# A rational activation's denominator without a square, and the order of its quotients, in a two-layer kernel

## The chip, the cores and the metric

One core of a Trainium2 chip. The metric is the time on the device of one execution, in microseconds: the median of several runs. The kernel before took 1278.8 us (three runs, 1276.81 to 1279.39).

## What is computed

The input x has 8192 rows of 192 numbers. A causal convolution of seven taps along the rows (taps from a softmax) comes first. Two layers of the same shape follow, each a product to 2048 hidden numbers, an activation, and a product back to 192. The first activation is h * sigmoid(1.702 h). The second is rational:

```
h = x @ w_in
P = a[0] + a[1]*h + a[2]*h*h + a[3]*h*h*h
Q = 1 + |b[0]|*|h| + |b[1]|*h*h
out = (P / (Q + 1e-6)) @ w_out
```

## The kernel before

The rows are cut into 16 blocks of T = 512 (NB = 16), the hidden numbers into 16 parts of 128 that are handled in NS = 8 steps of two parts, so that a tile of the activation is 128 x 1024. The engines' instructions stand in a fixed order, written out by hand; nothing reorders them.

Three PSUM tiles (`ps_h`) take turns for hidden products, transposes and maxima, and one (`ps_o`) for the output products. A hidden product (`h_product`, L361) splits both sides into high and low halves in f16: six matmuls of the full 128 rows (L371) and six of 64 rows (L381). `o_chunk` (L392) multiplies one 128-part of the activation with its weights, in f16 halves for layer 1 and in f32 for layer 2 (16 matmul instructions for two chunks, L403).

The second activation runs in these passes on each 128 x 1024 tile:

- `terms` (L463): on ScalarE pp = scale*h + bias (L470), sq = h*h (L471) and qq = |scale*h| (L472); on VectorE two passes (L473, L474) that make the cubic P - a[0] out of pp and the hidden product in PSUM. The second gives the PSUM tile back.
- `denominator` (L477): on VectorE qq = sq*scale + qq (L478).
- `log` (L482) and `inverse` (L485): on ScalarE Ln (L483), then a sigmoid of the negative (L486), which together give 1/(1 + qq).
- `quotient` (L488): on VectorE pp = (pp + a[0]) * qq (L489). Its result is what the output product of layer 2 takes.

A pass of the loop over j has two phases. `front_phase` (L564) goes through the eight steps: hidden product and gelu of layer 1 for block j+1 (L420), its high half on GpSimd (L427) and low half on VectorE (L433), hidden product and `terms` of layer 2 for block j, and late output chunks of block j-1. `back_phase` (L595) has the output products of layer 1 for block j+1, the logarithms, the transposed input of block j+3 and its convolution on GpSimd (L297 a product with a tap, L301 the addition), the sigmoids, and then the input of layer 2 for block j+1: `x2_natural` copies it from PSUM (L445, L447), `x2_red` takes its maximum (L452), TensorE broadcasts the maxima (`all_max`, L82), VectorE reduces them (L86), ScalarE writes the high halves (L304) and VectorE the low halves (L307), and `x2_scales` makes columns of scales (L314). The first output chunks of layer 2 end the phase, and the rest goes into lists that the next front phase empties. The end of the phase:

```
        inv(0), inv(1)
        quo(0)
        x2 = x2_natural(n1)
        red = x2_red(x2)
        ...
        inv(2), inv(3)
        scales(pm, sc)
        x2_split(n1, pt, sc)
        quo(1), quo(2), quo(3)
        inv(4), inv(5), inv(6), inv(7)
        chunks[0](), chunks[1]()
        late_pe.extend(chunks[2:])
        late_dve.extend(lambda i=i: quo(i) for i in range(4, NS))
```

In front step i one quotient of `late_dve` is issued before `terms`, and two chunks of `late_pe` after it. The last block has no front phase of its own (`last_phase`, L520): units of hidden product, `terms` and `denominator`, the late work of the block before among them, then the quotients of the first five units, the store of the block before (L498), the last three units, and its own chunks. pp and qq come from rings of eight tiles each, so pp of a block's unit i waits for the chunks of unit i in the block before.

Of the kernel before, what the change touches and what calls it, by code (L numbers as in the profile page):

```python
# [8 lines left out]
F32 = mybir.dt.float32  # L9
# [11 lines left out]
def kernel(  # L21
# [392 lines left out]
    def o2_chunk(n, i, k, g, groups=range(NG)):  # L414
        o_chunk(1, n, NS * k + i, ((g[:, k * T:(k + 1) * T], wo2[:, NS * k + i]),), groups)

    def gelu(n, ph, g=None):
        if g is None:
            g = p2.tile([P, 2 * T], F32, tag="g1", name="g1")
# [3 lines left out]
        return g  # L423

    def g1_high(n, g):
        hl = p2.tile([P, 2, 2 * T], F16, tag="hl", name="hl1", bufs=8)
# [27 lines left out]

    def x2_scales(sc):

        unit = sc[:, 2:3]
        mul(unit, sc[:, 0:1], cst[:, 3:4])
        mul(sc[:, 3:8], ab[:, 8:13], unit)
        mul(sc[:, 5:8], sc[:, 5:8], unit)  # L460
        mul(sc[:, 7:8], sc[:, 7:8], unit)

    def terms(n, ph):  # L463

        sc = sc2_t[n]
        pp = rings[0].tile([P, 2 * T], F32, tag="p", name="pp")
        qq = rings[0].tile([P, 2 * T], F32, tag="q", name="qq")
        sq = p2.tile([P, 2 * T], F32, tag="sq", name="sq")
# [5 lines left out]
        nc.vector.scalar_tensor_tensor(out=pp, in0=pp, scalar=sc[:, 3:4], in1=h, op0=ALU.add, op1=ALU.mult)  # L474
        return pp, qq, sq

    def denominator(n, qq, sq):  # L477
# [4 lines left out]
    def log(qq):  # L482
        nc.scalar.activation(out=qq, in_=qq, func=ACTF.Ln, bias=eps)  # L483

    def inverse(qq):  # L485
        nc.scalar.activation(out=qq, in_=qq, func=ACTF.Sigmoid, scale=-1.0)  # L486

    def quotient(n, pp, qq):  # L488
        nc.vector.scalar_tensor_tensor(  # L489
            out=pp, in0=pp, scalar=ab[:, 0:1], in1=qq, op0=ALU.add, op1=ALU.mult  # L490
        )

    def store(n):
        po = po_t.pop((1, n))
        sc2_t.pop(n)
        t = p1.tile([P, NG, D], F32, tag="on", name="on")
        for k in range(2):
            nc.scalar.activation(  # L498
                out=t[:, 2 * k:2 * k + 2], in_=po[:, k, 0:2 * D].rearrange("p (g d) -> p g d", g=2), func=ACTF.Copy
            )  # L500
        nc.sync.dma_start(out=out[n * T:(n + 1) * T].rearrange("(g p) d -> p g d", p=P), in_=t)
# [3 lines left out]
    def store_half(n, k):  # L505

        if k == 0:
            on_t[n] = p1.tile([P, NG, D], F32, tag="on", name="on")
        t = on_t[n][:, 2 * k:2 * k + 2]
        src = po_t[1, n][:, k, 0:2 * D].rearrange("p (g d) -> p g d", g=2)  # L510
        if k:
            nc.vector.tensor_copy(out=t, in_=src)
        else:
            nc.scalar.activation(out=t, in_=src, func=ACTF.Copy)
# [3 lines left out]
    late_pe, late_dve, early = [], [], {}  # L518

    def last_phase(j):  # L520

        fronts = []

        def units(i, late_q, late_o):
            ph = h_product(1, j, i)
            pp, qq, sq = terms(j, ph)
            for _ in range(late_q):
                late_dve.pop(0)()
            for _ in range(late_o):
                late_pe.pop(0)()  # L530
            denominator(j, qq, sq)
            fronts.append((pp, qq))

        def quotients(steps):
            for i in steps:
                log(fronts[i][1])
            for i in steps:
                inverse(fronts[i][1])
                quotient(j, *fronts[i])

        def own(i):
            for k in range(2):
                o2_chunk(j, i, k, fronts[i][0])

        first = NS // 2 + 1
        for i in range(first):
# [3 lines left out]
        units(first, 0, 0), units(first + 1, 0, 0)  # L550
        own(0)
        units(first + 2, 0, 0)
        for i in range(1, first):
            own(i)
        quotients(range(first, NS))
        for i in range(first, NS - 1):
            own(i)
        for groups in (range(0, 2), range(2, 4)):
            for k in range(2):
                o2_chunk(j, NS - 1, k, fronts[NS - 1][0], groups)  # L560
        store_half(j, 0)
        store_half(j, 1)

    def front_phase(j, n1, extras):  # L564

        fronts, splits = [], []
        for i in range(NS):
            if n1 is not None:
                g = gelu(n1, early.pop((n1, i), None) or h_product(0, n1, i))
                hl = g1_high(n1, g)  # L570
                splits.append(hl)
            if late_dve:
                late_dve.pop(0)()
            if j is not None:
                ph = h_product(1, j, i)
                pp, qq, sq = terms(j, ph)
            for _ in range(2):
                if late_pe:
                    late_pe.pop(0)()
            if n1 is not None:  # L580
                g1_low(n1, g, hl)
            if j is not None:
                denominator(j, qq, sq)
                fronts.append((pp, qq))
            for f in extras.get(i, ()):
                f()
        return fronts, splits
# [7 lines left out]
    def back_phase(j, n1, n2, conv, fronts, splits):  # L595

        for i in range(NS):
            if conv is not None and i == 0:
                x_transpose(conv)
                for k in range(K):  # L600
                    x_conv_pool(conv, k)
            if n1 is not None:
                o1_product(n1, i, splits[i])
            if fronts:
                log(fronts[i][1])
            if conv is not None:
                if i == 5:
                    x_max(conv)
                    x_scales(conv)
                    x_scale_out(conv)  # L610
        inv = lambda i: inverse(fronts[i][1])
        quo = lambda i: quotient(j, *fronts[i])
        chunks = [lambda i=i, k=k: o2_chunk(j, i, k, fronts[i][0]) for i in range(NS) for k in range(2)]
# [3 lines left out]
        inv(0), inv(1)  # L617
        quo(0)
        x2 = x2_natural(n1)
        red = x2_red(x2)  # L620
        sc = sc2_t[n1] = tiny.tile([P, 8], F32, tag="sc2", name="sc2")
        transposes(pt, x2)
        all_max(red, pm)
        inv(2), inv(3)
        scales(pm, sc)
        x2_split(n1, pt, sc)
        quo(1), quo(2), quo(3)
        inv(4), inv(5), inv(6), inv(7)
        chunks[0](), chunks[1]()
        late_pe.extend(chunks[2:])  # L630
        late_dve.extend(lambda i=i: quo(i) for i in range(4, NS))

    def prologue():
# [45 lines left out]
        for c, (src, func) in enumerate(((1, ACTF.Copy), (4, ACTF.Abs), (2, ACTF.Copy), (5, ACTF.Abs), (3, ACTF.Copy))):  # L679
            nc.scalar.activation(out=ab[:, 8 + c:9 + c], in_=ab[:, src:src + 1], func=func)  # L680
# [29 lines left out]
        for i in range(NS):  # L710
            hl = p2.tile([P, 2, 2 * T], F16, tag="hl", name="g0", bufs=8)
            g0.append(gelu(0, h_product(0, 0, i), hl.rearrange("p two t -> p (two t)").bitcast(F32)))
# [38 lines left out]
        sc = sc2_t[0] = tiny.tile([P, 8], F32, tag="sc2", name="sc2")  # L751
# [19 lines left out]
    with tc.manual_schedule():  # L771
        for j in range(NB):
# [16 lines left out]
            if n1 is None:  # L789
                last_phase(j)  # L790
                break
            fronts, splits = front_phase(j, n1, extras)
            back_phase(j, n1, n2, conv, fronts, splits)
# [27 lines left out]
```

## Time and profile before

| | |
|---|---|
| median of three runs | 1278.8 us (1276.81 to 1279.39) |
| the profiled execution | 1279.72 us |
| its span, first to last instruction | 1277.8 us |
| TensorE, matmuls busy | 1215.6 us |
| VectorE busy | 1028.3 us |
| ScalarE busy | 963.0 us |
| GpSimd busy | 606.5 us |

Busy times are of the span of the profiled execution. A matmul's end is modelled, so TensorE's busy time is not its time at the peak rate. An idle time in front of an instruction is put down to what released it last. In a row of the timeline "x16" means sixteen instructions of one line in a row, and the bracket is the engine's idle time before the first.

### The profile page before, as it was taken

Reading aid. Unit: us, or ns where it says so; the run is one execution under the profiler, and the core shown is the slowest. Engines: PE = TensorE matmul, PEld = TensorE weight load, DVE = VectorE, ACT = ScalarE, POOL = GpSimd, SP = SyncE. Lnnn points to the kernel's source line nnn. Section 1 sums busy time; section 2 is a strip of 40 time slices with the busy share of each in tenths; the row PEclk is TensorE's granted clock in tenths of the full one; section 3 lists DMA queues with packets and bytes.
Section 4 is the critical chain, followed back from the end, with each engine's and each line's share of the span. In section 5 each row is a group of like instructions: output and inputs, shape, how many; then the busy total and the mean of one; then the engine's idle time right before and its main releaser. Section 6 shows DMA issues by size and latency. Waiting matters only on the chain.

```text
span 1277.8 us, 20189 instructions
## 1 busy us (share of the span) xinstructions
PE 1215.6 (95%) x8538; PEld 852.8 (67%) x8538; DVE 1028.3 (80%) x1045; ACT 963.0 (75%) x989; POOL 606.5 (47%) x429
## 2 busy tenths in 40 slices
PE   5999999999999999899998999999999999999977
PEld 2564757757685766767676676866767586676766
DVE  6877898796969879696897969789696978968575
ACT  3626977869687786968778697877869787786876
POOL 2024654819365481927638284572928456312000
PEclk9999999999999999999999999999999999999999
DMA  7700001000010100001010010101001000000000
GB/s 230 231 17 1 1 1 30 1 15 16 1 30 1 31 1 24 7 1 30 1 30 1 1 30 1 30 1 29 1 1 30 1 14 1 13 1 12 2 1 25
DMA packets 31164, 28.57 MB, mean 22 GB/s; under 512 B 9825, under 2 KB 30305, under 8 KB 30305
## 3 DMA queue, kind: packets, MB, share of 16 engines
q1 hardware_dynamic: 30480, 27.27, 7.4%
q8 instruction: 67, 1.10, 0.4%
q14 instruction: 24, 0.20, 0.1%
q10 hardware_dynamic: 593, 0.01, 0.0%
HBM read 20.98 MB, written 6.29 MB: 21 GB/s over the span
## 4 chain that ended last, share of the span: by engine, by line
PE 52%; POOL 27%; DVE 10%; issue 5%; ACT 5%; DMA 1%; ACTq 0%; POOLq 0%; DVEq 0%
PE ph L371 19%; PE po L403 19%; POOL xc L301 15%; PE ph L381 10%; POOL tap L297 10%; PE pc L286 3%; DVE pp L489 2%; DVE qq L478 2%; DVE pp L473 2%; DVE pp L474 1%; PE pt L250 1%; POOL xc L297 1%; ACT sq L471 1%; POOL hl L427 1%; ACT qq L472 1%
## 5 line engine op out<-in xcount | busy, mean ns | idle before, releaser
L427 POOL TENSOR_SCALAR hl<-g,sc 128x1024 f16<-128x1024 f32 x120 | 199.0, 1660 | 462.1 <-ACT g L420 462.1
L371 PE MATMUL ph<-xs,wm 128*128 128x512 f16 x1536 | 376.2, 381 | 12.1 <-DVE pp L474 7.7
L403 PE MATMUL po<-wo,pp 128*128 128x192 f32 x2048 | 359.2, 330 | 24.7 <-DVE pp L489 24.7
L403 PEld LDWEIGHTS po<-wo,pp 128*128 128x128 f32 x2048 | 341.2, 192 | 45.6 <-DVE pp L489 32.8
L371 PEld LDWEIGHTS <-wm 128*128 128x128 f16 x1536 | 138.4, 98 | 202.1 <-issue 63.6
L420 ACT ACTIVATE g<-ph,sc 128x1024 f32<-128x1024 f32 x128 | 142.7, 1115 | 136.9 <-PE ph L381 114.3
L489 DVE SCALAR_TENSOR_TENSOR pp<-pp,ab,qq 128x1024 f32<-128x1024 f32 x128 | 206.2, 1642 | 46.9 <-ACT qq L486 46.9
L403 PE MATMUL po<-wo,hl 128*128 128x192 f16 x2880 | 242.2, 246 | 0.0
L403 PEld LDWEIGHTS <-hl 128*128 128x128 f16 x2880 | 238.5, 98 | 0.8
L470 ACT ACTIVATE pp<-ph,sc 128x1024 f32<-128x1024 f32 x128 | 154.3, 1206 | 99.2 <-PE ph L371 88.6
L301 POOL TENSOR_TENSOR xc<-xc,tap 128x1024 f32<-128x1024 f32 x78 | 224.8, 2882 | 6.5
L473 DVE TENSOR_TENSOR pp<-pp,ph 128x1024 f32<-128x1024 f32 x128 | 155.4, 1214 | 58.3 <-ACT qq L472 58.3
L381 PE MATMUL ph<-xs,wr 64*128 64x512 f16 x1536 | 195.1, 379 | 6.3 <-DVE xs L307 5.3
L433 DVE SCALAR_TENSOR_TENSOR hl<-g,sc,hl 128x1024 f16<-128x1024 f32 x120 | 177.5, 1479 | 10.9 <-POOL hl L427 10.9
L478 DVE SCALAR_TENSOR_TENSOR qq<-sq,sc,qq 128x1024 f32<-128x1024 f32 x128 | 172.4, 1347 | 0.0
L474 DVE SCALAR_TENSOR_TENSOR pp<-pp,sc,ph 128x1024 f32<-128x1024 f32 x128 | 163.9, 1280 | 4.5
L381 PEld LDWEIGHTS <-wr 64*128 64x128 f16 x1536 | 64.0, 94 | 126.1 <-issue 69.5
L297 POOL TENSOR_SCALAR tap<-xt,wt 128x512 f32<-128x512 f32 x156 | 144.1, 935 | 6.4
L472 ACT ACTIVATE qq<-ph,sc 128x1024 f32<-128x1024 f32 x128 | 143.0, 1117 | 0.0
L483 ACT ACTIVATE qq<-qq,eps 128x1024 f32<-128x1024 f32 x128 | 135.1, 1136 | 3.2 <-DVE qq L478 3.0
L471 ACT ACTIVATE sq<-ph 128x1024 f32<-128x1024 f32 x128 | 130.1, 1016 | 0.0
L486 ACT ACTIVATE qq<-qq 128x1024 f32<-128x1024 f32 x128 | 126.2, 1050 | 0.2
(85 smaller groups left out, 596.9 us busy)
## 6 DMA issues: line engine op xcount, KB each, us to landing
xn<-in_x_dram SPq DMA_DIRECT2D x16, 384.0 KB, 4.1
raw<-in_moe_w_out_dram SPq DMA_DIRECT2D x8, 768.0 KB, 7.0
out_dram<-on SPq DMA_DIRECT2D x15, 384.0 KB, 3.0
raw<-in_moe_w_in_dram SPq DMA_DIRECT2D x4, 1024.0 KB, 5.9
xn<-in_x_dram SPq DMA_DIRECT2D x16, 128.0 KB, 4.0
raw<-in_moe_w_in_dram SPq DMA_DIRECT2D x4, 512.0 KB, 7.9
out_dram<-on SPq DMA_DIRECT2D x2, 192.0 KB, 2.0
wt<-in_weight_dram ACTq DMA_DIRECT2D x2, 0.4 KB, 6.1
```

Source lines behind the costliest of these rows:

```text
L297: nc.gpsimd.tensor_scalar(out=d[:, j], in0=t[:, j, k:k + T], scalar1=wt[:, j, k:k + 1], scalar2=1.0, op0=ALU.mult, op1=ALU.mult)
L301: nc.gpsimd.tensor_tensor(out=c, in0=c, in1=d, op=ALU.add)
L371: nc.tensor.matmul(out=ph[:, k], lhsT=wm[m][:, a_, f], rhs=xs[:, 2 * b_], start=(first and q == 0), stop=(not first and q == 2),)
L381: nc.tensor.matmul(out=ph[:, k], lhsT=wr[m][rows, a_, f], rhs=xs[rows, 2 * b_ + 1], start=(first and q == 0), stop=(not first and q == 2),)
L403: nc.tensor.matmul(out=dst, lhsT=lhsT[:, g * P:(g + 1) * P], rhs=rhs, start=(done == 0 and g % 2 == 0 and q == 0), stop=(done == NF - 1 an ...
L427: nc.gpsimd.tensor_scalar(out=hl[:, 0], in0=g, scalar1=sc1_t[n][:, 4:5], scalar2=1.0, op0=ALU.mult, op1=ALU.mult)
L433: nc.vector.scalar_tensor_tensor(out=hl[:, 1], in0=g, scalar=sc1_t[n][:, 4:5], in1=hl[:, 0], op0=ALU.mult, op1=ALU.subtract)
L472: nc.scalar.activation(out=qq, in_=h, func=ACTF.Abs, scale=sc[:, 4:5])
L473: nc.vector.tensor_tensor(out=pp, in0=pp, in1=h, op=ALU.mult)
L474: nc.vector.scalar_tensor_tensor(out=pp, in0=pp, scalar=sc[:, 3:4], in1=h, op0=ALU.add, op1=ALU.mult)
L478: nc.vector.scalar_tensor_tensor(out=qq, in0=sq, scalar=sc2_t[n][:, 6:7], in1=qq, op0=ALU.mult, op1=ALU.add)
L489: nc.vector.scalar_tensor_tensor(out=pp, in0=pp, scalar=ab[:, 0:1], in1=qq, op0=ALU.add, op1=ALU.mult)
```

## The change

- The denominator is |b1| * |h| * (|h| + |b0/b1|). ScalarE writes qq = s*|h| (s is the scale back to true values), VectorE makes (qq + |b0/b1|) * qq, and the factor |b1| is the scale of the logarithm, taken from a column. The square and its tile go; |b1| and |b0/b1| are made once (`b_consts`). In `unit`, which takes the place of `terms`, Abs stands ahead of the linear pass.
- In the back phase quotient 1 stands ahead of `scales` on VectorE, and three chunks are issued at once for two.
- In front step i the late quotient 4 + i stands behind the two cubic passes and ahead of the low half; before it stood ahead of the cubic.
- The gelu tile has three buffers for two.
- The last block's pp lies in the eight f16 tiles of layer 1's activation (`hl`), which nothing else uses by then, and its late chunks are given out as 0, 0, 2, 5, rest.

The core of the diff:

```diff
+        nc.scalar.activation(out=ab[:, 8:14], in_=ab[:, 0:6], func=ACTF.Abs)
+        nc.vector.tensor_scalar(out=ab[:, 14:16], in0=ab[:, 12:14], scalar1=2.0 ** -80, scalar2=None, op0=ALU.max)
+        nc.vector.reciprocal(out=ab[:, 6:8], in_=ab[:, 14:16])
+        mul(ab[:, 14:15], ab[:, 12:13], ab[:, 7:8])
...
-        nc.scalar.activation(out=pp, in_=h, func=ACTF.Identity, scale=sc[:, 7:8], bias=sc[:, 5:6])
-        nc.scalar.activation(out=sq, in_=h, func=ACTF.Square)
-        nc.scalar.activation(out=qq, in_=h, func=ACTF.Abs, scale=sc[:, 4:5])
+        nc.scalar.activation(out=qq, in_=h, func=ACTF.Abs, scale=sc[:, 2:3])
+        nc.scalar.activation(out=pp, in_=h, func=ACTF.Identity, scale=sc[:, 7:8], bias=sc[:, 6:7])
...
-            out=qq, in0=sq, scalar=sc2_t[n][:, 6:7], in1=qq, op0=ALU.mult, op1=ALU.add
+            out=qq, in0=qq, scalar=ab[:, 14:15], in1=qq, op0=ALU.add, op1=ALU.mult
...
-        nc.scalar.activation(out=qq, in_=qq, func=ACTF.Ln, bias=eps)
+        nc.scalar.activation(out=qq, in_=qq, func=ACTF.Ln, scale=ab[:, 15:16], bias=eps)
...
 def last_phase(j):
+            pp = hl_tile().rearrange("p two t -> p (two t)").bitcast(F32)
+            unit(j, h_product(1, j, i), pp)
+            if i < first:
+                late_step(j - 1, i)
+            for _ in range(late):
                 late_pe.pop(0)()
+            denominator(j, i)
...
-            units(i, *((0, 0) if i < 2 else (1, 2) if i < first - 1 else (len(late_dve), len(late_pe))))
+        for i, late in enumerate((0, 0, 2, 5)):
+            units(i, late)
+        units(first - 1, len(late_pe))
...
 def front_phase(j, n1, extras):
-            if late_dve:
-                late_dve.pop(0)()
...
+            unit(j, h_product(1, j, i))
+            if j:
+                late_step(j - 1, i)
...
 def back_phase(j, n1, n2, conv, splits):
-        inv(2), inv(3)
+        each(inverse, j, (2, 3))
+        quotient(j, 1)
         scales(pm, sc)
         x2_split(n1, pt, sc)
-        quo(1), quo(2), quo(3)
-        inv(4), inv(5), inv(6), inv(7)
-        chunks[0](), chunks[1]()
-        late_pe.extend(chunks[2:])
-        late_dve.extend(lambda i=i: quo(i) for i in range(4, NS))
+        each(quotient, j, (2, 3))
+        each(inverse, j, (4, 5, 6, 7))
...
+        for f in chunks[:3]:
+            f()
+        late_pe.extend(chunks[3:])
```

## Rows read from the trace of the kernel before

**Rows 1.** The page, busy us (share of the span) and instructions of each engine

```profile
PE 1215.6 (95%) x8538; PEld 852.8 (67%) x8538; DVE 1028.3 (80%) x1045; ACT 963.0 (75%) x989; POOL 606.5 (47%) x429
```

**Rows 2.** Who waited for whom, whole span: us in total, times, longest

```profile
ACT g L420 <- PE ph L381: 114.3, 84, 3.9
...
PE po L403 <- DVE pp L489: 24.7, 18, 3.2
...
PE ph L371 <- DVE pp L474: 7.7, 11, 1.4
...
PE ph L381 <- DVE xs L307: 5.3, 15, 0.6
```

**Rows 3.** The same list, TensorE alone, from 1199 us to the end

```profile
PE po L403 <- DVE pp L489: 8.9, 4, 3.0
...
PE ph L381 <- DVE xs L307: 0.6, 1, 0.6
```

**Rows 4.** Two stretches: length, busy us of each engine, granted TensorE clock, DMA

```profile
540.00:550.00 10.00, 10.00 (x52) 7.18 (x51) 9.96 (x7) 5.27 (x6) 7.49 (x4) 0.83 0.00 0
690.00:700.00 10.00, 9.19 (x46) 6.71 (x47) 9.96 (x7) 5.44 (x6) 9.32 (x5) 0.83 0.01 2
```

**Rows 5.** Timeline of one passage: start us, us, engine, instruction, [idle before]

```profile
605.90 0.95 DVE L452 TENSOR_REDUCE red<-x2n 128x1 f32<-128x768 f32 x1 [0.50 <-ACT x2n L447]
...
607.89 2.77 PE L403 MATMUL po<-wo,pp 128*128 128x192 f32 x16
608.10 0.29 DVE L86 TENSOR_REDUCE top<-pm 128x1 f32<-128x128 f32 x1 [1.25 <-PE pm L82]
...
611.53 0.39 PE L381 MATMUL ph<-xs,wr 64*128 64x512 f16 x2 [0.33 <-DVE xs L307]
...
612.53 8.10 DVE L489 SCALAR_TENSOR_TENSOR pp<-pp,ab,qq 128x1024 f32<-128x1024 f32 x4
613.09 3.19 POOL L301 TENSOR_TENSOR xc<-xc,tap 128x1024 f32<-128x1024 f32 x1
...
614.13 2.87 PE L403 MATMUL po<-wo,pp 128*128 128x192 f32 x16 [0.81 <-DVE pp L489]
...
631.02 1.47 PE L371 MATMUL ph<-xs,wm 128*128 128x512 f16 x6 [0.62 <-DVE pp L474]
```

**Rows 6.** Timeline of another passage, from 535.4 to 538.5 us

```profile
535.49 2.34 POOL L301 TENSOR_TENSOR xc<-xc,tap 128x1024 f32<-128x1024 f32 x1
...
535.60 3.32 DVE L489 SCALAR_TENSOR_TENSOR pp<-pp,ab,qq 128x1024 f32<-128x1024 f32 x1
```

**Rows 7.** Groups of instructions: busy us, mean ns of one, idle before

```profile
L470 ACT ACTIVATE pp<-ph,sc 128x1024 f32<-128x1024 f32 x128 | 154.3, 1206 | 99.2 <-PE ph L371 88.6 <-PE po L403 8.6 <-POOL wo L188 2.1
...
L472 ACT ACTIVATE qq<-ph,sc 128x1024 f32<-128x1024 f32 x128 | 143.0, 1117 | 0.0
...
L471 ACT ACTIVATE sq<-ph 128x1024 f32<-128x1024 f32 x128 | 130.1, 1016 | 0.0
...
L680 ACT ACTIVATE ab<-ab 128x1 f32<-128x1 f32 x5 | 0.6, 187 | 0.0
```

**Rows 8.** Timeline of the last block

```profile
1210.64 1.22 DVE L473 TENSOR_TENSOR pp<-pp,ph 128x1024 f32<-128x1024 f32 x1 [1.03 <-ACT qq L472]
...
1238.69 1.15 ACT L483 ACTIVATE qq<-qq,eps 128x1024 f32<-128x1024 f32 x1 [1.46 <-DVE qq L478]
...
1245.90 0.84 ACT L498 ACTIVATE on<-po 128x384 f32<-128x384 f32 x2
...
1247.61 2.76 PE L403 MATMUL po<-wo,pp 128*128 128x192 f32 x16
...
1252.37 10.56 PE L403 MATMUL po<-wo,pp 128*128 128x192 f32 x64
...
1260.84 1.15 ACT L483 ACTIVATE qq<-qq,eps 128x1024 f32<-128x1024 f32 x1 [1.56 <-DVE qq L478]
...
1265.73 8.07 PE L403 MATMUL po<-wo,pp 128*128 128x192 f32 x48 [2.80 <-DVE pp L489]
```

More of the change, by code (lines that the diff above doesn't have):

```diff
@@ L465, in terms, with unit @@
+    def x2_scales(sc):
+        s = sc[:, 2:3]
+        mul(s, sc[:, 0:1], cst[:, 3:4])
+        mul(sc[:, 5:8], ab[:, 1:4], s)
+        mul(sc[:, 6:8], sc[:, 6:8], s)
+        mul(sc[:, 7:8], sc[:, 7:8], s)
+    units_t = {}
+    def unit(n, ph, pp=None):
         sc = sc2_t[n]
-        pp = rings[0].tile([P, 2 * T], F32, tag="p", name="pp")
+        if pp is None:
+            pp = rings[0].tile([P, 2 * T], F32, tag="p", name="pp")
         qq = rings[0].tile([P, 2 * T], F32, tag="q", name="qq")
-        sq = p2.tile([P, 2 * T], F32, tag="sq", name="sq")
@@ L491, in quotient, with each, late_step, out_tile @@
         )
+    def each(f, n, steps):
+        for i in steps:
+            f(n, i)
+    def late_step(n, i):
+        if i < NS // 2:
+            quotient(n, NS // 2 + i)
+    def out_tile(n, k):
+        return po_t[1, n][:, k, 0:2 * D].rearrange("p (g d) -> p g d", g=2)
     def store(n):
-        po = po_t.pop((1, n))
-        sc2_t.pop(n)
         t = p1.tile([P, NG, D], F32, tag="on", name="on")
@@ L564, in front_phase @@
     def front_phase(j, n1, extras):
-        fronts, splits = [], []
+        splits = []
         for i in range(NS):
[L568 to L571, printed above, removed]
-            if late_dve:
[L573 to L576, printed above, removed]
+            g = gelu(n1, early.pop((n1, i), None) or h_product(0, n1, i))
+            hl = g1_high(n1, g)
+            splits.append(hl)
+            unit(j, h_product(1, j, i))
+            if j:
+                late_step(j - 1, i)
             for _ in range(2):
@@ L579, in front_phase @@
                     late_pe.pop(0)()
[L580 to L584, printed above, removed]
+            g1_low(n1, g, hl)
+            denominator(j, i)
             for f in extras.get(i, ()):
                 f()
-        return fronts, splits
+        return splits
     def x2_split(n, pt, sc):
@@ L593, in x2_split, with back_phase @@
         x2_scales(sc)
-    def back_phase(j, n1, n2, conv, fronts, splits):
-        for i in range(NS):
[L598 to L613, printed above, removed]
+    def back_phase(j, n1, n2, conv, splits):
+        if conv is not None:
+            x_transpose(conv)
+            for k in range(K):
+                x_conv_pool(conv, k)
+        for i in range(NS):
+            o1_product(n1, i, splits[i])
+            log(j, i)
+            if conv is not None and i == 5:
+                x_max(conv)
+                x_scales(conv)
+                x_scale_out(conv)
         pt, pm = ps_tile("pt"), ps_tile("pm2")
@@ L678, in prologue @@
         w_in_split(0, slice(T, HALF))
-        for c, (src, func) in enumerate(((1, ACTF.Copy), (4, ACTF.Abs), (2, ACTF.Copy), (5, ACTF.Abs), (3, ACTF.Copy))):
-            nc.scalar.activation(out=ab[:, 8 + c:9 + c], in_=ab[:, src:src + 1], func=func)
+        b_consts()
         red1 = tiny.tile([P, 4], F32, tag="wred", name="wred")
@@ L710, in prologue @@
         for i in range(NS):
-            hl = p2.tile([P, 2, 2 * T], F16, tag="hl", name="g0", bufs=8)
-            g0.append(gelu(0, h_product(0, 0, i), hl.rearrange("p two t -> p (two t)").bitcast(F32)))
+            ph = h_product(0, 0, i)
+            g0.append(gelu(0, ph, hl_tile().rearrange("p two t -> p (two t)").bitcast(F32)))
             if i < 4:
@@ L750, in prologue @@
         red = x2_red(x2)
[L751 removed]
+        sc = sc2_t[0] = tiny.tile([P, 24], F32, tag="sc2", name="sc2")
         transposes(pt, x2)
@@ L771 @@
     with tc.manual_schedule():
-        for j in range(NB):
+        for j in range(NB - 1):
             n1, n2, conv = (j + d if j + d < NB else None for d in (1, 2, 3))
```

84 lines of the change are left out of this document (38 added, 46 removed).

## The prediction

> **What bounds the kernel now.** I read the page's busy shares first: TensorE is at 95% and VectorE at 80% [rows 1]. A busy share says nothing of who is late, so next came the list of who waits for whom, cut to TensorE. Three waits in it belong to the region that the change touches, and all three end on VectorE or its inputs: the second-layer output product waits for a quotient, a first matmul of the hidden product waits for the cubic's second pass to give a PSUM tile back, and the hidden product of layer 2 waits for the low half of its split input [rows 2]. The same list for the last 79 us shows how much of these belongs to the end of the kernel [rows 3]. So the steady part holds 24.7 - 8.9 = 15.8 us for quotients, 7.7 us for the cubic and 5.3 - 0.6 = 4.7 us for the split: 28.2 us in 13 to 14 passages from one block to the next. The longest single wait is 3.2 us, for a quotient, and in two stretches of ten microseconds the granted clock is 0.83: part of each ran at 1.2 instead of 2.4 GHz, which costs 10 x 0.17 = 1.7 us, 3.4 us together [rows 4]. The first of them lies just behind a quotient of 3.32 us [rows 6]. All else of a block is TensorE at work back to back, which the change doesn't touch. **At most 28.2 + 3.4 = 31.6 us** are to be had there, and some more in the last block.
>
> Then the timeline of one ordinary passage [rows 5]. The reader should see the order on VectorE: maximum of x2 (from 605.90), the reduction over the broadcast maxima (608.10, when the matmul before it has delivered), the low half (there at 611.53, when TensorE goes on), the scale products, and only then the second quotient (612.53). TensorE has had two chunks (from 607.89), idles 0.33 us for the low half, does the hidden product, and idles 0.81 us for quotient 1. Two steps later it idles 0.62 us for the cubic, because late quotients stand ahead of it. That is 1.76 us in a passage.
>
> **The change, part by part.**
>
> *Square goes, Abs feeds the denominator.* 128 instructions of 1.016 us leave ScalarE [rows 7]. ScalarE's gelu alone waited 114.3 us for TensorE [rows 2], so little of this is on the path; it lets the cubic start about 0.9 us earlier in a unit, since the cubic's wait ends on the last of the three ScalarE passes. The denominator stays one VectorE pass with two operands from SBUF, so I cost it at nothing; its bound is 0 to 0.1 us a pass, and it lies off the path but for the last block. The logarithm gains a scale taken from a column. From Square without such an operand to Abs with one, to the cubic's first pass with two, a pass grows by 0.10 and 0.09 us [rows 7]. I take 0.09 us for each logarithm, 0.7 us a block. Its cover is the Square that no longer stands ahead of the same chain (about 0.9 us); if that were gone, the maximum of x2 would start up to 0.7 us late.
>
> *Constants in the prologue.* Five ScalarE passes of 0.187 us [rows 7] become one, and three column-sized VectorE operations come. Within 1 us either way; I take 0.
>
> *Quotient 1 ahead of the scales, a third chunk at once.* VectorE is free between the end of the maximum, 605.90 + 0.95 = 606.85, and 608.10, so 1.25 us of a quotient cost nothing. Four of them took 8.10 us, and with 3.3 us for the one that met an addition 1.6 us remain for each of the others: the reduction comes 0.35 us later, and I take 0.5, since a tap product can be in the way as well. TensorE now has three chunks (4.0 us from 607.89, to 611.9) before the hidden product, where it had two (to 610.6). The low half, due at 611.5 + 0.5 = 612.0, is wanted only by the last matmuls of the product's first part, at 612.4: the 0.33 us goes. The product ends at 614.1 and chunk 3 at 615.4, whose quotient has long been there: the 0.81 us goes too. **Late next is quotient 2**, for chunk 4. It starts when the scale products are done, at 612.53 + 0.5 = 613.0, and GpSimd's convolution runs beside it. Nothing in the trace shows quotient 2 in this place, so I bound it. Not hindered it takes 1.6 us and is there at 614.6: no wait. If it meets a GpSimd addition, it takes what a quotient took that began beside one, 3.32 us [rows 6]: to 616.3, a wait of 0.9 us. If the low half is another microsecond late as well, the wait is 1.8 us. I take 0.9 us, since an addition began at 613.09 [rows 5], just there, and GpSimd's work keeps its order. Ends: 0 and 1.8 us.
>
> *Late quotients behind the cubic.* In steps 0 to 3 the cubic's two passes come 1.2 us sooner, which more than covers the 0.62 us. What is queued behind them on VectorE: the low half of the gelu split and the denominator, each wanted only in the back half of the block. The moved quotients 4 to 7 feed chunks 8 to 15, which TensorE comes to two steps later: no new wait. A third gelu tile lets ScalarE go on where it waited for that low half; that is off the path.
>
> *Queues.* The store, the loads on SP and GpSimd's instructions stand where they stood; the change moves no transfer past another.
>
> *The last block.* Here GpSimd is idle, and VectorE is the bound [rows 8]. The first cubic pass started at 1210.64; without Square and with the reduction 0.3 us later it starts at 1210.0. Cubic (two passes), late quotient and denominator are four passes of 1.22 us, about 4.85 us as their starts follow each other, four times, and the fifth unit 3.65 us: the fifth denominator ends at 1233.1, where the logarithm that waited for it started at 1238.69. That is 5.6 us sooner, because pp has tiles of its own and ScalarE no longer waits for TensorE. The store's copies, which ended at 1245.90 + 0.84 = 1246.74, follow and end at 1241.2, and this is what the block's own chunks wait for: 1241.2 for 1247.61. TensorE needs 15.3 us from there to the last step (1252.37 + 10.56 - 1247.61), to 1256.5. VectorE has three units more from 1243.4 on (11.0 us), to 1254.4, and from the last denominator to the last chunks it took 1265.73 - 1260.84 = 4.9 us: 1259.3. The last chunks start at 1259.3 instead of 1265.73: **6.4 us**. Bounds: 3 us if the new idle time ahead of 1241 brings the lower clock on the path, and 7 us.
>
> **Sum.** The profiled execution took 1279.7 us (span 1277.8), 0.9 us above the median of the runs, 1278.8. 31.6 - 13 x 0.9 + 6.4 = 26.3 us less: 1253.4 us, and 1252.5 us against the median.
>
> **Where a page speaks against it.** The row shows a quotient of 3.32 us that began 0.1 us after a GpSimd addition of 2.34 us [rows 6], so the two did not run side by side. The Trainium skill, "SBUF — State Buffer", section "Who interferes with whom", says that a VectorE instruction with two operands from SBUF and a GpSimd instruction that reads SBUF exclude each other for a whole instruction, and that the one which starts first wins. The trace bears this out in that row. By it quotient 1, now ahead of the reduction, can hold up the whole chain of x2 by an addition, which is the third rival.
>
> **The rivals.**
> 1. *Nothing waits any more.* Quotient 2 is never hindered: 31.6 + 6.4 = 38.0 us, 1240.8. For it: in the passage of rows 5 quotient 1 slipped in ahead of an addition, with a TensorE wait of only 0.81 us. Against it: the two long waits. Chance 0.14.
> 2. *The wait only moves.* Each passage keeps 1.76 us, behind quotient 2: 31.6 - 22.9 + 6.4 = 15.1 us, 1263.7. Chance 0.14.
> 3. *Slower: quotient 1 stands behind an addition ahead of the reduction.* It then ends at 606.85 + 3.32 = 610.2, the reduction is 2.1 us late, and so are high and low half: TensorE idles 0.3 + 0.7 us in the hidden product, and 1.4 us for quotient 2 if that meets an addition too: 2.4 us. If such idle time brings the lower clock each time, as the 3.2 us did, 1.7 us more: 4.1 us a passage. 31.6 - 53.3 + 6.4 = 15.3 us more, 1294.1. It decides from 38.0 / 13 = 2.9 us a passage. Against it: the first quotient now goes ahead of its addition, so the second would meet the short products between additions. Chance 0.07.
> 4. *The change doesn't do what it says:* 2.4 us a passage at full clock, and the last block's tiles are not free in time. 31.6 - 31.2 = 0.4 us, 1278.4. Chance 0.05.
>
> **How the numbers follow.** The forecast has 0.60 (1246 to 1260). The range of 1239 to 1266 takes in it and the first two rivals, and leaves out 0.12. Within 0.2%, about what a measurement of this kernel can tell from no change, lies only the fourth: 0.05. Faster by more: 0.60 + 0.14 + 0.14 = 0.88. Slower: 0.07.
>
> **What would show it.** Right: no wait of TensorE for the low half, nor for the cubic in step 2; one wait of a passage on chunk 4 for a quotient, under 1.8 us; no granted clock under 1 in the steady part; a block period of 73 to 74 us; the last chunks about 6 us sooner, relative to the last maximum. Wrong: a reduction over the maxima that starts over 2 us after its matmul, with a quotient of 3 us ahead of it, or a steady period above 74.3 us.

## The result, and the profile after

The changed kernel takes 1261.6 us, the kernel before in the same set of runs 1279.1: a ratio of 0.9865, 95% interval 0.9846 to 0.9884. That is 17.5 us less, where 26.3 were forecast. The profiled execution took 1262.3 us, its span 1260.5. First the page's busy times, and of the list of who waited for whom the rows that answer to [rows 2, 3]; in the new lines L506 is the quotient, L525 the store's copies.

```profile
PE 1211.6 (96%) x8538; PEld 852.6 (68%) x8538; DVE 1062.8 (84%) x1048; ACT 860.2 (68%) x857; POOL 601.3 (48%) x429
```

```profile
PE po L403 <- DVE pp L506: 18.5, 12, 1.6
...
PE po L403 <- ACT on L525: 4.2, 1, 4.2
...
PE ph L381 <- DVE xs L307: 0.4, 1, 0.4
```

ScalarE is busy 103 us less than before and VectorE 34.5 us more [rows 1]. TensorE's waits for the cubic are gone, those for the low half all but gone, and one kind is left in the steady part: twelve waits for a quotient, 18.5 us, most of them 1.57 us long. The block period is 74.0 us, where it was 74.3 in an ordinary block and 77.5 in the two that had the long wait. So an ordinary block gained only 0.26 us. The timeline of one shows why (compare [rows 5]):

```profile
598.46 2.35 POOL L301 TENSOR_TENSOR xc<-xc,tap 128x1024 f32<-128x1024 f32 x1
598.80 3.10 DVE L506 SCALAR_TENSOR_TENSOR pp<-pp,ab,qq 128x1024 f32<-128x1024 f32 x1 [1.78 <-ACT qq L502]
...
601.82 0.94 DVE L456 TENSOR_REDUCE red<-x2n 128x1 f32<-128x768 f32 x1
602.68 1.52 DVE L506 SCALAR_TENSOR_TENSOR pp<-pp,ab,qq 128x1024 f32<-128x1024 f32 x1
...
603.13 4.07 PE L403 MATMUL po<-wo,pp 128*128 128x192 f32 x24
...
604.12 0.28 DVE L86 TENSOR_REDUCE top<-pm 128x1 f32<-128x128 f32 x1
...
607.92 2.67 DVE L314 TENSOR_SCALAR sc<-sc 128x2 f32<-128x2 f32 x2
607.95 2.36 POOL L301 TENSOR_TENSOR xc<-xc,tap 128x1024 f32<-128x1024 f32 x1
...
610.50 3.30 DVE L506 SCALAR_TENSOR_TENSOR pp<-pp,ab,qq 128x1024 f32<-128x1024 f32 x2
...
612.22 1.57 PE L403 MATMUL po<-wo,pp 128*128 128x192 f32 x8 [1.57 <-DVE pp L506]
```

Read it from below. TensorE waits for quotient 2, the first of the pair that starts at 610.50. That pair stands behind the last two scale products, which together took 2.67 us from 607.92, and a GpSimd addition ran for just that time. A scale product of two columns takes 0.23 us where no addition stands beside it. By its record the first of the two products started 0.03 us ahead of the addition, and still it was the one that was held. Above it is a second collision: quotient 0 started 0.34 us into an addition, took 3.10 us, and the maximum of x2 (601.82) followed late. Before the change the same quotient came just ahead of its addition. Here are its rows in the passage of [rows 5], with the hidden product that TensorE begins there, and that hidden product after the change:

```profile
604.01 1.39 DVE L489 SCALAR_TENSOR_TENSOR pp<-pp,ab,qq 128x1024 f32<-128x1024 f32 x1 [1.95 <-ACT qq L486]
604.41 3.22 POOL L301 TENSOR_TENSOR xc<-xc,tap 128x1024 f32<-128x1024 f32 x1
...
604.60 1.46 PE L371 MATMUL ph<-xs,wm 128*128 128x512 f16 x6
```

```profile
599.55 1.46 PE L371 MATMUL ph<-xs,wm 128*128 128x512 f16 x6
```

TensorE began its chunks 1.99 us behind the start of the maximum before (607.89 - 605.90) and 1.31 us behind it after (603.13 - 601.82): against TensorE, the maximum now comes 0.68 us later.

The groups of instructions show that the held scale product is the rule: sixteen of them with a mean of 1.87 us, of which the timeline shows twelve held, each 2.4 us, in the twelve passages with the wait, and the first two and last two at 0.2 us. The second row below is the logarithm, with its scale from a column.

```profile
L498 ACT ACTIVATE qq<-qq,eps,ab 128x1024 f32<-128x1024 f32 x128 | 146.9, 1229 | 1.0 <-DVE qq L492 0.8
...
L314 DVE TENSOR_SCALAR sc<-sc 128x2 f32<-128x2 f32 x16 | 29.9, 1869 | 0.6
```

In the rows of stretches (length, busy us of each engine, granted clock, DMA) a steady block now runs at full clock; its longest wait is 1.57 us. Two stretches outside do not:

```profile
537.20:611.30 74.10, 72.43 (x532) 51.77 (x532) 64.74 (x61) 52.48 (x53) 44.47 (x31) 1.00 0.05 13
59.00:64.00 5.00, 5.00 (x23) 5.00 (x22) 4.23 (x9) 3.78 (x6) 0.00 (x0) 0.66 0.55 174
1229.00:1234.00 5.00, 3.66 (x14) 3.67 (x15) 4.40 (x5) 5.00 (x7) 0.00 (x0) 0.66 0.24 79
```

The last block, to be held against [rows 8]:

```profile
1198.69 1.22 DVE L486 TENSOR_TENSOR hl<-hl,ph 128x1024 f32<-128x1024 f32 x1 [1.31 <-ACT hl L485]
...
1229.44 0.84 ACT L525 ACTIVATE on<-po 128x384 f32<-128x384 f32 x2
...
1230.34 4.28 PE L403 MATMUL po<-wo,hl 128*128 128x192 f32 x16 [4.23 <-ACT on L525]
...
1243.47 1.24 ACT L498 ACTIVATE qq<-qq,eps,ab 128x1024 f32<-128x1024 f32 x1 [0.76 <-DVE qq L492]
...
1248.45 8.07 PE L403 MATMUL po<-wo,hl 128*128 128x192 f32 x48 [1.27 <-DVE hl L506]
```

From the first cubic pass to the last chunks it is 49.8 us, where it was 55.1. By the stretches between the gelus that open a block, where the time went: the 14 blocks from the first to the last of them 12.9 us less (1043.3 to 1030.4), the last stretch 7.3 less (140.6 to 133.3), the prologue 3.0 more (93.9 to 96.8). 12.9 + 7.3 - 3.0 = 17.2. Of the 12.9 us, 6.9 come from the two blocks that had the long wait, 2.8 from the second of the 14 and 1.3 from the last. In the prologue the clock took 1.7 us of the 3.0: the same 48 matmuls before (first row) and after, in the stretch of 0.66 shown above:

```profile
56.76 7.97 PE L403 MATMUL po<-v,g 128*128 128x192 f32 x48
```

```profile
58.03 9.65 PE L403 MATMUL po<-v,hl 128*128 128x192 f32 x48
```

### The profile page after: what moved, and what is told of

Same layout as the page of the kernel before. It is cut to its first block, busy times and chain, and to the rows that moved or that the text cites. A ratio compares the mean times of both kernels' runs of the same rounds, so it can differ in the third digit from the quotient of the medians.

```text
span 1260.5 us, 19971 instructions
## 1 busy us (share of the span) xinstructions
PE 1211.6 (96%) x8538; PEld 852.6 (68%) x8538; DVE 1062.8 (84%) x1048; ACT 860.2 (68%) x857; POOL 601.3 (48%) x429
## 4 chain that ended last, share of the span: by engine, by line
PE 59%; ACT 20%; DVE 16%; POOL 2%; issue 2%; DMA 1%; ACTq 0%; POOLq 0%; DVEq 0%
PE ph L371 23%; PE po L403 21%; PE ph L381 12%; ACT qq L498 10%; DVE pp L506 6%; PE pc L286 3%; DVE sc L314 3%; ACT qq L502 2%; ACT L502 1%; DVE xs L307 1%; ACT L498 1%; ACT pp L485 1%; ACT xs L304 1%; ACT qq L484 1%; POOL xc L301 1%
## 5 line engine op out<-in xcount | busy, mean ns | idle before, releaser
L431 POOL TENSOR_SCALAR hl<-g,sc 128x1024 f16<-128x1024 f32 x120 | 181.5, 1514 | 460.7 <-ACT g L421 460.6
L403 PE MATMUL po<-wo,pp 128*128 128x192 f32 x1920 | 334.2, 327 | 18.5 <-DVE pp L506 18.5
L403 PEld LDWEIGHTS po<-wo,pp 128*128 128x128 f32 x1920 | 316.9, 190 | 36.6 <-DVE pp L506 22.1
L403 PE MATMUL po<-wo,hl 128*128 128x192 f16 (+1 forms) x3008 | 265.1, 250 | 5.5 <-ACT on L525 4.2
L506 DVE SCALAR_TENSOR_TENSOR pp<-pp,ab,qq 128x1024 f32<-128x1024 f32 x120 | 201.9, 1692 | 38.0 <-ACT qq L502 38.0
L492 DVE SCALAR_TENSOR_TENSOR qq<-qq,ab 128x1024 f32<-128x1024 f32 x128 | 180.7, 1411 | 0.0
L486 DVE TENSOR_TENSOR pp<-pp,ph 128x1024 f32<-128x1024 f32 x120 | 145.3, 1211 | 25.8 <-ACT pp L485 25.8
L487 DVE SCALAR_TENSOR_TENSOR pp<-pp,sc,ph 128x1024 f32<-128x1024 f32 x120 | 153.7, 1281 | 4.3
L498 ACT ACTIVATE qq<-qq,eps,ab 128x1024 f32<-128x1024 f32 x128 | 146.9, 1229 | 1.0 <-DVE qq L492 0.8
L485 ACT ACTIVATE pp<-ph,sc 128x1024 f32<-128x1024 f32 x120 | 143.8, 1198 | 0.0
L86 DVE TENSOR_REDUCE top<-pm 128x1 f32<-128x128 f32 x35 | 10.0, 286 | 69.5 <-PE pm L82 69.5
```

The source lines that it names most:

```text
L403: nc.tensor.matmul(out=dst, lhsT=lhsT[:, g * P:(g + 1) * P], rhs=rhs, start=(done == 0 and g % 2 == 0 and q == 0), stop=(done == NF - 1 an ...
L431: nc.gpsimd.tensor_scalar(out=hl[:, 0], in0=g, scalar1=sc1_t[n][:, 4:5], scalar2=1.0, op0=ALU.mult, op1=ALU.mult)
L492: nc.vector.scalar_tensor_tensor(out=qq, in0=qq, scalar=ab[:, 14:15], in1=qq, op0=ALU.add, op1=ALU.mult)
L498: nc.scalar.activation(out=qq, in_=qq, func=ACTF.Ln, scale=ab[:, 15:16], bias=eps)
L506: nc.vector.scalar_tensor_tensor(out=pp, in0=pp, scalar=ab[:, 0:1], in1=qq, op0=ALU.add, op1=ALU.mult)
```

## The experiments

The kernel before took 1275.2 to 1279.5 us in the different sets of runs, while kernels with the changed kernel's steady blocks came out at 1261.0 to 1262.6 in the three sets that hold one (the set of the first four experiments holds none); so I compare medians in us, and the block periods of the profiles, with the ratio to the kernel before beside them. A difference of medians under 2 us between sets says nothing by itself. Theory A: a scale product held by a GpSimd addition, with quotient 2 queued behind it, sets the wait.

**Quotient 2 ahead of the scale products.**

```diff
         low(pt, sc[:, 1:2], xs)
-        x2_scales(sc)
...
         x2_split(n1, pt, sc)
-        each(quotient, j, (2, 3))
+        quotient(j, 2)
+        x2_scales(sc)
+        quotient(j, 3)
...
         x2_split(0, pt, sc)
+        x2_scales(sc)
```

> The changed kernel with one move: quotient 2 stands ahead of the scale products of x2, not behind them. Theory A (in each passage the one wait left, 1.57 us on chunk 4, comes from a scale product of two columns that took 2.42 us beside a GpSimd addition, and quotient 2 queued behind it): quotient 2 starts at the low half's end, about 3 us sooner and ahead of that addition; 12 waits of 1.57 us go, 18.8 us, so about 1243 us, and a steady period of 72.4 to 72.6 us. Theory B (VectorE's load sets the passage, the scale product only stood in the way by chance): another wait of TensorE on VectorE takes its place, less than 6 us gained, 1256 to 1262 us.

1240.5 us, ratio 0.9722 (0.9707 to 0.9736), 21.1 us less than the changed kernel. The list has no wait of TensorE in a steady passage any more, and the period is 72.2 us. The timeline of a passage:

```profile
598.32 1.53 DVE L506 SCALAR_TENSOR_TENSOR pp<-pp,ab,qq 128x1024 f32<-128x1024 f32 x1
...
598.87 3.20 POOL L301 TENSOR_TENSOR xc<-xc,tap 128x1024 f32<-128x1024 f32 x1
...
600.02 2.08 DVE L314 TENSOR_SCALAR sc<-ab,sc 128x3 f32<-128x3 f32 x1
```

Quotient 2 began 0.55 us ahead of the addition and took 1.53 us; the addition took 3.20 us for 2.35. A scale product is still held, now one of three columns, but no wait of TensorE stands behind it. Quotient 0 is held here too (3.12 us in this passage, as in the changed kernel), without a wait of TensorE for a quotient. Theory B falls.

**The scale products one column at a time.**

```diff
-        mul(sc[:, 5:8], ab[:, 1:4], s)
-        mul(sc[:, 6:8], sc[:, 6:8], s)
-        mul(sc[:, 7:8], sc[:, 7:8], s)
+        for c in range(3):
+            for k in range(c + 1):
+                mul(sc[:, 5 + c:6 + c], sc[:, 5 + c:6 + c] if k else ab[:, 1 + c:2 + c], s)
```

> The changed kernel with the scale products of x2 made one column at a time: seven small products where there were four, same order of everything else. Theory A in its narrow form (only products of more than one column are held by a GpSimd addition; those of one column took 0.2 us beside one): the products end about 608.9 us in the passage where they ended at 610.6; quotient 2 itself is then held by the addition to about 611.4, so the wait on chunk 4 falls from 1.57 to about 0.75 us: 10 us less, about 1252 us. Rival (any column product is held by an addition): wait as before or longer by the added products, 1261 to 1266 us.

1253.3 us, ratio 0.9821 (0.9805 to 0.9838), period 73.26 us, and twelve waits of 0.8 us at the most:

```profile
603.44 2.36 POOL L301 TENSOR_TENSOR xc<-xc,tap 128x1024 f32<-128x1024 f32 x1
603.50 0.21 DVE L314 TENSOR_SCALAR sc<-sc 128x1 f32<-128x1 f32 x1
603.63 0.20 DVE L314 TENSOR_SCALAR sc<-ab,sc 128x1 f32<-128x1 f32 x1
603.87 0.46 DVE L314 TENSOR_SCALAR sc<-sc 128x1 f32<-128x1 f32 x2
604.25 4.26 DVE L506 SCALAR_TENSOR_TENSOR pp<-pp,ab,qq 128x1024 f32<-128x1024 f32 x2
...
606.93 1.57 PE L403 MATMUL po<-wo,pp 128*128 128x192 f32 x8 [0.80 <-DVE pp L506]
```

Four products of one column run inside the addition at 0.2 us each. More instructions, and 8.3 us less: in the same place a product of one column is not held and one of two columns is. What is left is quotient 2, which started 0.81 us into the addition and was held by it.

**Quotient 1 back behind the split, two chunks at once.**

```diff
-        for i, late in enumerate((0, 0, 2, 5)):
+        for i, late in enumerate((0, 0, 3, 5)):
...
         each(inverse, j, (2, 3))
-        quotient(j, 1)
         scales(pm, sc)
         x2_split(n1, pt, sc)
-        each(quotient, j, (2, 3))
+        each(quotient, j, (1, 2, 3))
...
-        for f in chunks[:3]:
+        for f in chunks[:2]:
...
-        late_pe.extend(chunks[3:])
+        late_pe.extend(chunks[2:])
```

> The changed kernel with one part undone: quotient 1 again behind the split and the scale products, two chunks at once instead of three (14 late chunks, given out in the last block as 0, 0, 3, 5, rest). If that part is what the steady passages gained by: the wait of 0.33 us for the low half returns and chunk 2 waits for quotient 1, which stands behind the held scale product: 2 to 3 us of idle TensorE a passage for the 1.57 us, so 6 to 20 us more, 1268 to 1281 us. If the order of quotient 1 is worth little (the wait only moves with it): within 3 us of 1261.6.

1296.5 us, ratio 1.0156 (1.0135 to 1.0176): worse than expected, and slower than the kernel before. The wait for the low half is back (0.33 us), and chunk 2 waits:

```profile
619.27 2.35 POOL L301 TENSOR_TENSOR xc<-xc,tap 128x1024 f32<-128x1024 f32 x1
619.29 2.60 DVE L314 TENSOR_SCALAR sc<-sc 128x2 f32<-128x2 f32 x2
...
623.53 2.71 PE L403 MATMUL po<-wo,pp 128*128 128x192 f32 x15 [2.81 <-DVE pp L506]
```

The same held product, with nothing to cover it. The wait of 2.81 us stands in twelve passages. Behind four of them the clock fell as well, and those blocks took 77.4 to 77.5 us where the others took 75.8. The new place of quotient 1 and the third chunk, undone together here, are what makes the other parts bearable.

**Late quotients ahead of the cubic again.**

```diff
-            unit(j, h_product(1, j, i))
+            ph = h_product(1, j, i)
             if j:
                 late_step(j - 1, i)
+            unit(j, ph)
```

> The changed kernel with one part undone: in each front step the late quotient stands ahead of the cubic again. If this move is what took away the 0.62 us for the cubic in step 2: up to 12 waits of 0.6 us come back, 1265 to 1270 us. If the shorter ScalarE part of a unit did that by itself (the square gone, the cubic starting sooner): within 2 us of 1261.6.

1263.1 us, ratio 0.9906, period 74.05 us. One wait for the cubic came back, 2.0 us in the first passage, and none in the twelve others. This move is worth about 2 us, once: the 14 blocks took 2.2 us more in the profile, the median was 1.5 us up.

**A Square put back**, in the changed kernel and in the one with quotient 2 first.

```diff
         nc.scalar.activation(out=qq, in_=h, func=ACTF.Abs, scale=sc[:, 2:3])
+        sq = p1.tile([P, 2 * T], F32, tag="sq", name="sq")
+        nc.scalar.activation(out=sq, in_=h, func=ACTF.Square)
         nc.scalar.activation(out=pp, in_=h, func=ACTF.Identity, scale=sc[:, 7:8], bias=sc[:, 6:7])
```

> The changed kernel with a Square of the hidden product put back on ScalarE between the absolute value and the cubic's first pass; its result goes to a tile that nothing reads, and the denominator stays as changed. Theory C (the square's 1.0 us was off TensorE's path in the steady part, since ScalarE waits for TensorE in each step): 1260 to 1264 us. Theory D (it was on the path at the end of each passage, where the eight logarithms, now 1.13 us apart, let the second sigmoid end 0.04 us before the copy of x2 starts, so that anything added ahead of them delays that copy): the copy comes 0.9 us later and TensorE waits for it: 0.4 to 0.9 us more in 12 passages, 1266 to 1273 us.

> The same Square put back, but in the kernel with quotient 2 ahead of the scale products (72.2 us a block, 1240.5 on this measure). Theory C: 72.2 us a block still, 1239 to 1243 us. Theory D: 0.4 to 0.9 us more a block, 1246 to 1253 us, with TensorE waiting for the copy of x2.

1276.9 us (0.9975) and 1255.2 us (0.9816): 15.3 and 14.7 us more, and more than Theory D had (1266 to 1273, 1246 to 1253). The period grew by 0.95 us in the first (74.97) and by 0.9 in the second (73.1), and the last stretch by 2.3 and 4.3. In the timeline of the first, TensorE waits for the maximum of x2:

```profile
603.52 2.36 POOL L301 TENSOR_TENSOR xc<-xc,tap 128x1024 f32<-128x1024 f32 x1
...
603.68 1.46 PE L371 MATMUL ph<-xs,wm 128*128 128x512 f16 x6
...
603.84 3.12 DVE L508 SCALAR_TENSOR_TENSOR pp<-pp,ab,qq 128x1024 f32<-128x1024 f32 x1 [2.69 <-ACT qq L504]
...
607.88 0.49 PE L82 MATMUL pm<-ident,red 128*128 128x128 f32 x2 [0.97 <-DVE red L456]
```

Theory D in kind: the Square was on the path at the end of a block, though the size was missed. The first rows show something that the forecast didn't look at. With the Square put back, quotient 0 and the addition that meets it both come 0.9 us later against the hidden product (0.16 us behind it and 0.16 ahead of it, where they were 0.75 and 1.09 ahead). So the Square moves GpSimd's additions as well as the quotient. The traces of the two kernels show how: the convolution's first product starts 0.16 to 0.17 us behind the end of ScalarE's copy of the transposed input (L266), which stands on ScalarE right behind the passes of the last unit. Before the change (first rows) that copy began 13.76 us ahead of the hidden product of 604.60, after it 14.67 us ahead of that of 599.55; with the Square put back it is 13.76 again.

```profile
590.84 1.03 ACT L266 ACTIVATE xt<-pt 128x1024 f32<-128x1024 f32 x1
...
592.03 1.36 POOL L297 TENSOR_SCALAR xc<-xt,wt 128x512 f32<-128x512 f32 x2 [1.51 <-issue]
```

```profile
584.88 1.02 ACT L266 ACTIVATE xt<-pt 128x1024 f32<-128x1024 f32 x1
...
586.07 1.36 POOL L297 TENSOR_SCALAR xc<-xt,wt 128x512 f32<-128x512 f32 x2 [0.68 <-POOL xt L265]
```

**The logarithm's scale as an immediate.**

```diff
-        nc.scalar.activation(out=qq, in_=qq, func=ACTF.Ln, scale=ab[:, 15:16], bias=eps)
+        nc.scalar.activation(out=qq, in_=qq, func=ACTF.Ln, scale=1.0, bias=eps)
```

> The changed kernel with the logarithm's scale an immediate 1.0 instead of a column, so the factor |b1| is left out of the denominator. Eight logarithms should end 0.7 us sooner. If ScalarE's chain (logarithms, table, two sigmoids) sets where quotient 0 meets GpSimd: quotient 0 starts ahead of the addition that held it for 3.1 us, the maximum of x2 starts 0.8 us sooner, and the scale products end before the addition that held them: the wait on chunk 4 falls from 1.57 us to between 0 and 0.9 us, 8 to 19 us less, 1243 to 1254 us. If the phase is set elsewhere: the wait stays, 1260 to 1263 us.

This kernel leaves the factor |b1| out, so it isn't a kernel to use. 1236.8 us, ratio 0.9696 (0.9680 to 0.9713): 24.8 us less, beyond the expectation. No steady passage holds a wait of TensorE but one of 0.7 us, and the period is 71.9 us. The mean of a logarithm and the start of quotient 0:

```profile
L498 ACT ACTIVATE qq<-qq,eps 128x1024 f32<-128x1024 f32 x128 | 135.2, 1136 | 0.8 <-DVE qq L492 0.6
```

```profile
587.59 1.40 DVE L506 SCALAR_TENSOR_TENSOR pp<-pp,ab,qq 128x1024 f32<-128x1024 f32 x1 [1.04 <-ACT qq L502]
588.00 3.20 POOL L301 TENSOR_TENSOR xc<-xc,tap 128x1024 f32<-128x1024 f32 x1
...
589.08 1.46 PE L371 MATMUL ph<-xs,wm 128*128 128x512 f16 x6
```

0.093 us a logarithm, 0.74 us a block. The addition starts 1.08 us ahead of the hidden product (1.09 in the changed kernel); only the quotient has moved, to 0.41 us ahead of the addition, and it takes 1.40 us for 3.10. All that follows on VectorE comes sooner, and the scale products end ahead of the next addition. A kernel that keeps |b1| without a column for the logarithm was not tried.

**The last block's pp in the ring again**, and, in another kernel, **its late work given out as before**, with the free tiles kept.

```diff
-            pp = hl_tile().rearrange("p two t -> p (two t)").bitcast(F32)
-            unit(j, h_product(1, j, i), pp)
+            unit(j, h_product(1, j, i))
```

> The changed kernel with one part undone: the last block's pp in the ring of eight again, not in the free f16 tiles, so that a unit's first pass waits for the chunks of the same unit of the block before. If the tiles are what moved the last block (7.3 us shorter than before): the waits of ScalarE for TensorE come back, 5 to 7 us more, 1266 to 1269 us, and only the last block longer. If the missing square and the quotients did it: under 2 us more.

```diff
-            if i < first:
-                late_step(j - 1, i)
+            for q in {2: (0,), 3: (1,), 4: (2, 3)}.get(i, ()):
+                late_step(j - 1, q)
...
-        for i, late in enumerate((0, 0, 2, 5)):
+        for i, late in enumerate((0, 0, 2, 2)):
```

> The changed kernel with the last block's late work given out as before the change: late quotients in units 2, 3 and 4 instead of 0 to 3, and late chunks 0, 0, 2, 2, rest instead of 0, 0, 2, 5, rest. The free tiles are kept. The ring of pp was worth nothing there; if the earlier late quotients and chunks are what shortened the last block by 7.3 us: it is 3 to 6 us longer, 1265 to 1268 us. If that was the missing square and the third early chunk: within 1.5 us of 1261.6.

1261.4 us (0.9858) and 1262.6 us (0.9899); the last stretch 134.05 and 133.01 us, against 133.32. In the first, ScalarE does wait for TensorE again, from 1190 us on:

```profile
ACT pp L485 <- PE po L403: 5.2, 3, 2.5
```

but the end hardly moves. Neither part alone made the last block shorter.

**The constants at the end of the prologue**, and **two gelu tiles** instead of three.

```diff
         w_in_split(0, slice(T, HALF))
-        b_consts()
...
+        b_consts()
         out2_whole(2)
```

> The changed kernel with the constants of the denominator made at the end of the prologue, behind its last weight split, not in its middle. In the profiles the prologue was 1.2 to 3.0 us longer than before in each kernel with the new constants. If their three VectorE operations, which wait for ScalarE in the middle of the weight work, are the cause: 1 to 3 us less, 1258.5 to 1260.5 us, and a prologue of 94 us. If it is the landing of the first load and the granted clock, which differ from run to run: within 0.8 us of 1261.6, prologue 95 to 97 us.

```diff
-            g = p2.tile([P, 2 * T], F32, tag="g1", name="g1", bufs=3)
+            g = p2.tile([P, 2 * T], F32, tag="g1", name="g1")
```

> The changed kernel with two gelu tiles again instead of three. If the third is off the path, as the prediction had it: within 1.5 us of 1261.6. If it is what took away the 0.62 us for the cubic in step 2 (two gelu tiles made ScalarE wait for VectorE's low half, and the moved late quotient did not do it alone): up to 0.6 us in 12 passages, 1264 to 1269 us.

1261.2 us (0.9858) and 1261.0 us (0.9888): neither counts. The prologue of the first was 93.8 us in its profile, but its median is that of the others; over the profiles of the other changed kernels the prologue was 94.8 to 96.8 us. So what the constants cost, at most 2 or 3 us, is not settled, and the medians show none of it.

**The fastest that keeps the whole computation:** quotient 2 first, and in the last block the sixth unit ahead of the first logarithms and the store's copies between the sigmoids.

```diff
-        units(first - 1, len(late_pe))
-        quotients(range(first))
-        store(j - 1)
-        units(first), units(first + 1)
+        units(first - 1)
+        units(first, len(late_pe))
+        quotients(range(first), lambda: store(j - 1))
+        units(first + 1)
         own(0)
...
```

> Quotient 2 ahead of the scale products, and in the last block: the sixth unit ahead of the first group's logarithms (its hidden product ahead of the late chunks), and the copies of the store of the block before between the first two and the other three sigmoids. The passages as in the kernel with quotient 2 first (0.972 of the time before). In the last block VectorE's 4.0 us of idle time ahead of the first sigmoid hold the sixth unit's 3.65 us, and the block's own chunks start 2.8 us sooner: 3 to 4 us less, 0.969 to 0.970 of the time before. If TensorE or the lower clock becomes the bound at the end instead: under 1.5 us less, 0.971 or more.

1238.4 us, ratio 0.9709 (0.9695 to 0.9724), 2.1 us less than with quotient 2 first alone, in another set of runs, so that this is hardly clear of noise. In the profile the last stretch fell by 1.1 us (133.3 to 132.3), not by 3 to 4. An idle time of 3.55 us ahead of the block's own chunks is left (4.2 with quotient 2 first alone), and 16 matmuls behind it took 4.55 us, where they had taken 2.76 in [rows 8]:

```profile
1205.93 4.55 PE L403 MATMUL po<-wo,hl 128*128 128x192 f32 x16 [3.55 <-ACT on L525]
```

## Why the prediction was right, and where it was off

The sign, the range and the place were right: faster, 1239 to 1266, with one wait per passage on chunk 4, behind quotient 2, a period of 73 to 74 us (74.0) and no lower clock in the steady part. The size was not: 17.5 us for 26.3. At 1261.6 us the result lies outside the 1246 to 1260 that the forecast itself had, and beside the second rival's 1263.7, in which the wait only moves. The steady part gained by the two long waits and their clock, and hardly by the ordinary passages, where 1.76 us of idle TensorE became 1.57. In the terms of the sum, for the profiled executions: the steady waits are 18.5 us for the 13 x 0.9 = 11.7 forecast (6.8 us missing), the prologue is 3.0 us longer for 0, and the last block gave 7.3 us for 6.4. Together these make 8.9 us; the forecast missed the medians by 8.8. Step by step:

- *Quotient 1 and the third chunk.* Right. The waits of 0.33 and 0.81 us went, and the undone version shows how much hung on it in the changed kernel: 35 us, the lower clock of some passages included.
- *Quotient 2 is late next: 0.9 us.* **This is the term that was mis-sized: 1.57 us, in 12 passages.** On VectorE two errors cancelled, by luck. The forecast had quotient 2 start 7.1 us behind the start of the maximum (613.0 - 605.90), be held by an addition, and be there at 10.4 (616.3). It started at 8.7 (610.50 - 601.82), because I moved the scale products as a block of fixed length, and one of two columns was held for 2.4 us. But then the quotient was not held, and TensorE went on at 10.4. What made the wait longer is the other end: TensorE came to chunk 4 at 8.8 us behind the start of the maximum, not at 9.5, since the maximum had fallen 0.68 us back against TensorE. 0.9 + 0.68 makes 1.58, for the 1.57 measured. That the wait of 0.8 us with one column at a time is close to 0.9 is chance too: TensorE is as early there, and the quotient is held for less long.
- *The logarithm's scale, 0.09 us each, off the path.* The price was right (1.229 - 1.136 = 0.093 us). **The step that failed is "Its cover is the Square that no longer stands ahead of the same chain".** Against TensorE the cover held: quotient 0 starts 0.75 us ahead of the hidden product, where it started 0.59 ahead. Against GpSimd it didn't, for the additions came 0.9 us sooner as well (1.09 us ahead for 0.19). Between quotient and addition the logarithms' 0.74 us counted in full: from 0.40 us ahead of the addition to 0.34 us into it, in each of the twelve passages. Undone, it gives 24.8 us. The additions follow because the convolution starts on a copy that ScalarE makes behind the same Squares: the one cover moved both sides of the race.
- *The square: little on the path.* Wrong in its size. Put back, it costs about 0.95 us a block. Of the eight Squares of a block, 1.016 us each, about one counts, which fits with how little of the 103 us came through.
- *Late quotients behind the cubic: 0.62 us.* That wait went, but not by this move alone, nor by the third gelu tile or the missing square alone: with any one of them undone it stays away, but for one wait of 2.0 us. It has more than one remedy in the change.
- *The last block: 6.4 us.* Right in size (7.3 by the stretch, 6.1 from the last maximum to the last chunks, 5.3 from the first cubic pass), with the idle time ahead of the own chunks that was forecast (4.2 us). The lower clock that the bound of 3 us named did come behind it (16 matmuls in 4.28 us for 2.76), but the last chunks still waited 1.27 us for VectorE, so it was not on the path. The reason given, tiles of its own for pp, is not shown: the ring alone brings back 0.7 us, the old order of late work nothing, the square 2.3. The ring and the old order undone together were not tried, so what made up the sum stays open.
- *Prologue 0.* In its profile it is 3.0 us longer, 1.7 of them by the clock; over the profiles of the other kernels with the constants in the same place it is 0.9 to 2.8 us longer. The medians don't settle what the constants cost.

The rule quoted in the forecast reached further than I took it: the Trainium skill, "SBUF — State Buffer", section "Who interferes with whom", names products with a scalar among the instructions that can take the shared ports, and "VectorE: DVE Perf Modes", section "Mode 2×_2P — use both read ports for one tensor", says when one source is read through both: in SBUF, with an outermost non-unit dimension that is even, or odd and equal for source and result. The trace agrees: two and three columns were held for 2.4 and 2.1 us; of a single column the section says nothing, and the trace has it at 0.2 us beside an addition. That the one which starts first wins can't be read from starts so close together: in all twelve places the held product's record begins 0.03 us ahead of the addition's. On the logarithm, the Trainium skill, "ScalarE: Activation LUTs", section "What ACT_TABLE_LOAD costs", gives about 93 ns for each operand taken from a column; the trace has 93.

## What to carry to other kernels

Where VectorE and GpSimd share a stretch, list every VectorE instruction there, the column-sized ones too, and ask what it costs if a GpSimd instruction begins at about the same time; then put the one that another engine waits for ahead of those that only have to be done by and by. A tenth of a microsecond on a chain that decides who comes first is priced by the collision, not by its own length; and a cover has to hold against each engine that the chain meets, not only against the one that waits in the end. And undo parts one at a time: one part here was worth 35 us, another cost 25, and the sum of 17 shows neither.

## What was not expected of the hardware

A product of two columns, 0.2 us of work, took 2.4 us beside an addition of 2.36 us, while products of one column ran inside such an addition undisturbed. And the pattern is stable: the waits of 1.56 to 1.57 us repeat in eleven passages to 0.01 us, and quotient 0 starts 0.33 to 0.34 us into its addition in all twelve. The engines come to the same collision in every block.
